# A short convolution ahead of a gated network: another start-up order, a band from 38 small matmuls, and another last store

## The chip, the cores and the metric

The kernel runs on one core of one Trainium2 chip. The metric is the device time of one execution in microseconds (us), as the median of several runs. A ratio is the mean time of one kernel's fast runs over that of the other's of the same rounds on the same chip, so it is not quite the ratio of the medians that stand beside it. Verdicts use 2% as the border between "same" and "faster" or "slower".

## The reference, cut to what matters

```python
w = softmax(weight, axis=-1)                    # 8 heads x 7 taps
# causal depthwise convolution over the sequence, one row of taps for each 24 channels
out = einsum('hk,bskhg->bshg', w, windows_of(x_pad))      # x: (8, 4160, 192)
x = out.reshape(33280, 192)
h = maximum(maximum(x @ w1, x @ w2), x @ w3)    # 192 -> 768
return h @ w_out                                # 768 -> 192, float32
```

## The kernel before

The 33,280 tokens are cut into 65 blocks of 512. For each block the kernel loads x, casts it to fp16, does the convolution as 40 small matmuls against a banded matrix (`band`), copies the result out of PSUM, repacks it by six DMAs, doubles it into the other 64 partitions by one more, and then runs two stages. The *first stage* is six steps: a step is six matmuls into two PSUM banks (w1-w3 and w2-w3), a relu on ACT and a maximum on DVE. The *second stage* multiplies the six h tiles, and the convolved x itself through the small matrix m16, into the output. Blocks 0 and 1 are started in another way, by a dense convolution of 120 matmuls (`conv_dense`) that needs no repacking.

The parts that the change touches are the band, the order of the loads, the order of the first blocks, and the last stores:

```python
wk = const.tile([1, NHEAD * KW], FP32)          # the 56 taps on one partition
load_x(0)
... w in six pieces (three of them, a third of the columns, first) ...
load_x(1)
nc.sync.dma_start(out=wos[:], ...)
for t in range(2, 6):
    load_x(t)
...
nc.tensor.matmul(wps, lhsT=ones[:], rhs=wk[:], ...)       # taps onto 128 partitions
... exp, sum, reciprocal, product; seven shifted products on DVE ...
for k in range(KW):                                       # seven 304-column matmuls
    nc.tensor.matmul(ps[:], lhsT=ident16[:], rhs=shifted[:, k, :, :], ...)
... casts of x0 and copies of w3 on ACT ...
for a in range(4):
    nc.scalar.copy(out=band[32 * a:32 * a + 32, :, 32 * a:32 * a + WIN], in_=ps[...])
...
for t in range(1, NB):                                    # the loop starts at block 1
    load_x(t + 7); cast_x(t + 5); double(t + 2)
    l1(t, 0)
    ... convolutions of two blocks in every second iteration, copies, repack ...
    st2(t - 1, 0, NJ)
    for j in range(1, NJ):                                # first and second stage interleaved
        l1(t, j)
        st2(t - 1, j, NJ)
    store(t - 1, 0, 4, (nc.gpsimd,))
for u in range(NJ):
    st2(NB - 1, u, NJ)                                    # with the last block's stores
```

The softmax here doesn't subtract the row's maximum and nothing guards it: scores larger than these inputs give would overflow.

## Time and profile before

| what | value | from |
|---|---|---|
| time | 483.85 us (483.21 to 484.04, 3 runs) | times |
| span of the profiled run, mean granted clock | 480.0 us, 0.993 | profile |
| first convolution starts | 10.75 us | chain in order of time |
| convolutions of the iteration of block 4 | 47.99 us | chain in order of time |
| two blocks of the loop | 13.95 us | 61.94 - 47.99, the same chain |
| last add on DVE ends | 474.16 + 0.35 = 474.51 us | timeline |

A time in the profile counts from the start of the span. "PE" is TensorE; a line number names a line of that kernel's own file, so the convolution of blocks 0 and 1 is L342 in one kernel and L310 in another; the tile (`D`) is the same. The lines that the prediction rests on are shown there. One more place of the profile of before is needed: its end. The timeline's columns are start, duration, engine, line, operation, tiles.

```profile
474.16 0.35 DVE L436 TENSOR_TENSOR o<-a,po 128x192 f32<-128x192 f32 x1 [0.17 <-ACT a L435]
474.55 0.66 ACTq L452 DMA_DIRECT2D out_dram<-o  x1
```

The last arithmetic ends at 474.51, and the span ends 5.49 us later.

### The profile page before, as it was taken

Reading aid. Unit: us, or ns where it says so; the run is one execution under the profiler, and the core shown is the slowest. Engines: PE = TensorE matmul, PEld = TensorE weight load, DVE = VectorE, ACT = ScalarE, POOL = GpSimd, SP = SyncE. Lnnn points to the kernel's source line nnn. Section 1 sums busy time; section 2 is a strip of 40 time slices with the busy share of each in tenths; the row PEclk is TensorE's granted clock in tenths of the full one; section 3 lists DMA queues with packets and bytes.
Section 4 is the critical chain, followed back from the end, with each engine's and each line's share of the span. In section 5 each row is a group of like instructions: output and inputs, shape, how many; then the busy total and the mean of one; then the engine's idle time right before and its main releaser. Section 6 shows DMA issues by size and latency. Waiting matters only on the chain.

```text
span 480.0 us, 21944 instructions
## 1 busy us (share of the span) xinstructions
PE 468.4 (98%) x9083; PEld 393.7 (82%) x9083; DVE 365.8 (76%) x609; ACT 327.1 (68%) x608; POOL 211.3 (44%) x341
## 2 busy tenths in 40 slices
PE   7899999999999999999999999999999999999994
PEld 3578888888888888888888888888888888888994
DVE  6667877778777877877787787778777777778774
ACT  5676667676666767666666766676676767667663
POOL 2654534553454355445435544543545354345210
PEclk9899999999999999999999999999999999999998
DMA  8877756665766665566666657566556666644312
GB/s 198 216 188 209 214 147 194 173 187 160 202 168 181 184 184 165 162 196 179 173 179 185 171 155 196 168 189 178 170 158 191 186 169 176 179 126 135 112 44 95
DMA packets 67603, 82.08 MB, mean 171 GB/s; under 512 B 9424, under 2 KB 55760, under 8 KB 67504
## 3 DMA queue, kind: packets, MB, share of 16 engines
q1 hardware_dynamic: 53934, 49.01, 40.6%
q0 software_dynamic: 13216, 31.38, 18.4%
q8 instruction: 71, 1.16, 1.1%
q10 hardware_dynamic: 354, 0.30, 0.2%
q14 instruction: 28, 0.23, 0.1%
HBM read 30.31 MB, written 25.56 MB: 116 GB/s over the span
## 4 chain that ended last, share of the span: by engine, by line
PE 96%; ACT 1%; DVE 1%; issue 0%; POOL 0%; POOLq 0%
PE lp L383 32%; PE po L426 30%; PE lq L383 26%; PE G L322 7%; PE D L342 1%; PE idle L196 1%; ACT r L387 0%; PE band_sum L245 0%; ACT band L268 0%; ACT w3h L262 0%; DVE h L388 0%; DVE xz L216 0%; PE pm L305 0%; PE wps L223 0%; DVE band L218 0%
## 5 line engine op out<-in xcount | busy, mean ns | idle before, releaser
L388 DVE TENSOR_TENSOR h<-r,lq 128x512 f16<-128x512 f16 x390 | 266.9, 685 | 101.8 <-ACT r L387 101.8
L387 ACT ACTIVATE r<-lp 128x512 f16<-128x512 f32 x390 | 232.7, 597 | 135.0 <-PE lp L383 89.8
L383 PE MATMUL lp<-yd,wd 64*128 64x512 f16 x1170 | 315.4, 376 | 0.1
L383 PE MATMUL lq<-yd,wd 64*128 64x512 f16 x1170 | 314.6, 375 | 0.0
L426 PE MATMUL po<-wo,h 64*128 64x192 f16 x3120 | 231.3, 243 | 0.1
L426 PEld LDWEIGHTS <-h 64*128 64x128 f16 x3120 | 186.9, 94 | 26.1 <-issue 0.3
L383 PEld LDWEIGHTS <-wd 64*128 64x128 f16 x2340 | 164.4, 94 | 20.9 <-issue 1.4
L452 POOL DMA_DIRECT2D out_dram<-o x64 | 50.7, 792 | 245.9 <-DVE o L436 229.1
L366 POOL DMA_DIRECT2D yd<-ys x189 | 95.5, 509 | 2.2 <-ACT ys L353 1.4
L426 PE MATMUL po<-m,yd 64*128 64x192 f16 x780 | 86.8, 243 | 0.0
L436 DVE TENSOR_TENSOR o<-a,po 128x384 f32<-128x384 f32 (+1 forms) x132 | 71.3, 541 | 0.6 <-ACT a L435 0.6
L146 POOL CAST x<-xf 112x960 f16<-112x960 f32 x62 | 61.6, 995 | 2.3 <-DMA xf<-in_x_dram 2.3
L435 ACT COPY a<-po 128x384 f32<-128x384 f32 (+1 forms) x132 | 61.8, 469 | 1.2 <-PE po L426 1.2
L426 PEld LDWEIGHTS <-yd 64*128 64x128 f16 x780 | 55.0, 94 | 8.1
L322 PEld LDWEIGHTS <-x 112*32 112x32 f16 x2480 | 30.0, 97 | 13.3 <-issue 13.1
L353 DVE CAST ys<-G 128x512 f16<-128x512 f32 x60 | 38.4, 681 | 0.0
L353 ACT CAST ys<-G 128x512 f16<-128x512 f32 x66 | 35.8, 589 | 2.2 <-PE G L322 0.9
L322 PE MATMUL G<-band,x 112*32 112x103 f16 (+1 forms) x2480 | 35.0, 210 | 0.0
L161 POOL CAST xz<-xf 112x240 f16<-112x240 f32 (+2 forms) x6 | 2.4, 450 | 11.3 <-DMA xf<-in_x_dram 11.3
L196 PE MATMUL idle<-idle 128*128 128x512 f16 x14 | 5.7, 546 | 1.2 <-DVE unit L212 1.2
L342 PE MATMUL D<-band,xz 112*32 112x103 f16 (+1 forms) x240 | 4.1, 240 | 1.0 <-ACT band L268 1.0
L342 PEld LDWEIGHTS <-xz 112*32 112x32 f16 x240 | 3.8, 114 | 1.5 <-issue 1.4
(50 smaller groups left out, 41.2 us busy)
## 6 DMA issues: line engine op xcount, KB each, us to landing
out_dram<-o POOLq DMA_DIRECT2D x64, 384.0 KB, 3.9
xf<-in_x_dram SPq DMA_DIRECT2D x57, 420.0 KB, 4.8
yd<-yd SPq DMA_DIRECT2D x63, 192.0 KB, 3.2
yd<-ys SPq DMA_DIRECT2D x63, 48.0 KB, 3.6
yd<-ys POOLq DMA_DIRECT2D x63, 48.0 KB, 3.3
xf<-in_x_dram SPq DMA_DIRECT2D x8, 252.0 KB, 3.1
yd<-ys SPq DMA_DIRECT2D x63, 32.0 KB, 3.2
yd<-ys POOLq DMA_DIRECT2D x63, 32.0 KB, 2.9
```

What stands on the lines that cost most here:

```text
L146: nc.gpsimd.tensor_copy(out=v[0:rl, q0:q1, :], in_=xf[0:rl, q0:q1, :])
L322: nc.tensor.matmul(G[i][32 * g:32 * g + 32, lo:hi], lhsT=x16[0:rlen, cb:cb + 32], rhs=band[0:rlen, h, cc:cc + hi - lo], start=True, stop=T ...
L342: nc.tensor.matmul(ps[32 * g:32 * g + 32, lo:hi], lhsT=xz[t][0:rlen, q, v, 32 * s:32 * s + 32], rhs=band[0:rlen, h, cc:cc + hi - lo], star ...
L353: copy(out=slots[t][:, i, :], in_=convs[t][i][:])
L366: (nc.sync, nc.gpsimd)[n % 2].dma_start(out=yd[r0:r0 + rows, c, :], in_=slots[t][s0:s0 + rows, half, :])
L383: nc.tensor.matmul(ps[i][:, 0:N], lhsT=wd[row, c, P * j:P * (j + 1)], rhs=y[row, c, 0:N], start=(c == 0), stop=(c == NC - 1))
L387: nc.scalar.activation(out=r[:, 0:N], in_=ps[0][:, 0:N], func=AF.Relu)
L388: nc.vector.tensor_max(out=hs[t][:, j, 0:N], in0=r[:, 0:N], in1=ps[1][:, 0:N])
L426: nc.tensor.matmul(ps[b0, i][:, s % 2, :], lhsT=a, rhs=b, start=first, stop=last)
L435: nc.scalar.copy(out=a[:, ss, :], in_=ps[s0, 0][:, ss, :])
L436: nc.vector.tensor_add(out=outs[t][:, s0:s + 1, :], in0=a[:, ss, :], in1=ps[s0, 1][:, ss, :])
L452: qs[i].dma_start(out=bass.AP(tensor=out.tensor, offset=r * D, ap=[[D, n], [step * D, s1 - s0], [1, D]]), in_=ob[p0:p0 + n, s0:s1, :])
```

## The change

The intent is to start real work earlier and to keep TensorE on the blocks that are already there: the band comes from 38 matmuls of 8 columns instead of seven DVE products and seven 304-column matmuls; x1 is loaded behind the first third of w; second stages 0 and 1 both run ahead of block 2; loads of x are issued one at a time, with four buffers instead of six; and the last store but one leaves through SP in two halves. The cuts leave out smaller changes that come with these: w is loaded and copied in thirds, the casts of x0 move from ACT to DVE and those of w3 to GpSimd, and the second stage of block 0 takes its terms in another order.

```diff
-    xfp = ctx.enter_context(tc.tile_pool(name="xfp", bufs=6))
+    xfp = ctx.enter_context(tc.tile_pool(name="xfp", bufs=4))
...
     load_x(0)
-    ... w in six pieces on two queues ...
+    load_w(0)
     load_x(1)
+    load_w(1)
+    load_w(2)
     nc.sync.dma_start(out=wos[:], ...)
-    for t in range(2, 6):
-        load_x(t)
+    load_x(2)
...
-    keep_warm(2)
-    nc.tensor.matmul(wps[:]..., lhsT=ones[:], rhs=wk[:], start=True, stop=True)
-    ... taps, shifted (7 products) ...
-    keep_warm(7)
-    for k in range(KW):
-        nc.tensor.matmul(ps[:], lhsT=ident16[:], rhs=shifted[:, k, :, :], ...)
-    keep_warm(3)
+    keep_warm(6)
+    nc.scalar.activation(out=wexp[:], in_=wk[:], func=AF.Exp, accum_out=wsum[:])
+    nc.vector.reciprocal(out=wrec[:], in_=wsum[:])
+    nc.vector.tensor_scalar(out=line[:, 31:31 + KW], in0=wexp[:], scalar1=wrec[:], ...)
+    for c in range(WIN):
+        nc.tensor.matmul(bps[:, c, :], lhsT=line[:, WIN - 1 - c:WIN + 31 - c],
+                         rhs=ident16[0:NHEAD, 0:NHEAD], start=True, stop=True)
+    keep_warm(4)
...
+    conv_dense(0, ...)
+    l1(0, 0); l1(0, 1); conv_dense(1, ...); l1(1, 0); l1(1, 1); l1(0, 2); l1(0, 3)
+    load_x(3, nc.scalar)
+    ... the other steps of blocks 0 and 1, st2(0, 0) ...
+    conv(2, PQ); evac(2, ...); repack(2)
+    load_x(4)
+    ... st2(0, 1) to st2(0, 3), l1(1, 5) ...
+    double(2)
+    cast_x(3)
+    conv(3, PQ); evac(3, ...)
+    load_x(5)
+    repack(3)
+    ... rest of st2(0), then all six of st2(1) ...
+    load_x(6); double(3)
-    for t in range(1, NB):
+    for t in range(2, NB):                     # block 2 without second-stage work between
...
+            if t == NB - 1 and j == 3:
+                store(t - 1, 0, 2, (nc.sync,))
+        if t == NB - 1:
+            store(t - 1, 2, 4, (nc.sync,))
-        store(t - 1, 0, 4, (nc.gpsimd,))
+        elif t > 2:
+            store(t - 1, 0, 4, (nc.gpsimd,))
```

## The prediction

> **What bounds the kernel now.** I read the page first (chain of work, 40 slices), then the windows of each engine, then the timeline of the first 48 us and of the last 13, because the change touches only those ends. The page's chain of work that ended last, by engine, and its slices of TensorE and granted clock:
>
> ```profile
> PE 96%; ACT 1%; DVE 1%; issue 0%; POOL 0%; POOLq 0%
> ...
> PE   7899999999999999999999999999999999999994
> ...
> PEclk9899999999999999999999999999999999999998
> ```
>
> TensorE owns 96% of the chain. Only the first two slices (24 us) and the last hold idle time. The windows (length, then busy us and instruction count of PE, PEld, DVE, ACT, POOL, then clock, DMA share, GB/s) say it in numbers:
>
> ```profile
> 0.00:10.70 10.70, 7.28 (x21) 3.06 (x22) 7.04 (x18) 5.40 (x13) 2.97 (x18) 1.00 0.84 196
> 10.70:33.10 22.40, 20.51 (x529) 13.97 (x530) 13.24 (x22) 15.10 (x26) 12.95 (x21) 0.92 0.78 192
> ...
> 47.10:466.90 419.80, 419.69 (x8143) 358.49 (x8139) 328.93 (x542) 292.23 (x542) 187.74 (x291) 1.00 0.59 170
> ```
>
> From 47 us to 467 us TensorE is busy 419.69 of 419.80 us, so nothing there can be won, and the diff leaves those matmuls as they are. So I predict the time at which a fixed milestone is reached: the first-stage matmuls of block 4 start, with convolutions 0 to 6, first stages 0 to 3 and second stages 0 to 2 done. Before, that is at 47.1 us (timeline; the two convolutions of that iteration follow at 47.92). The difference at this milestone, plus the tail, is the whole change.
>
> Real work starts late and then stutters. From the chain in order of time (start, us, what):
>
> ```profile
> 7.24 1.79 PE band_sum L245 x7
> 9.05 0.40 ACT band L268
> 9.46 0.40 ACT band L268
> 9.88 0.40 ACT band L268
> 10.29 0.41 ACT band L268
> 10.75 1.55 PE D L342 x107
> ...
> 14.71 1.47 ACT w3h L262
> 16.20 0.60 ACT r L387
> ```
>
> The first convolution starts at 10.75, when the fourth band copy ends; later a 1.47 us cast on ACT delays a relu and TensorE waits.
>
> A second limit matters. One first-stage step (six matmuls) takes TensorE 0.64 us, but its two PSUM banks come free only after the relu (0.60) and the max (0.69): in the timeline a step begins at 456.20 and its max ends at 458.36, 2.16 us. With two banks of each kind, steps without second-stage work between them run at about 2.16/2 = 1.1 us. In the loop second-stage matmuls (about 0.41 us per step) fill that hole, so a loop step takes 1.06.
>
> [...] the granted clock is 0.81, 0.50 and 0.84 in the 2 us windows from 18, 20 and 22 us, which is (0.38+1.00+0.32)/0.5 = 3.4 us at half rate. [...] Here the six 64-column transposes beginning at 17.57 took 0.33 us with latency[...]. [...] Here even the small pieces take 3 us and more from issue to landing:
>
> ```profile
> xf<-in_x_dram SPq DMA_DIRECT2D x57, 420.0 KB, 4.8
> yd<-yd SPq DMA_DIRECT2D x63, 192.0 KB, 3.2
> ...
> yd<-ys POOLq DMA_DIRECT2D x63, 48.0 KB, 3.3
> ```
>
> **The change part by part.**
>
> *Band.* Removed: ones, the K=1 product, the replicated exp, seven DVE products (2.79 us) and seven 304-column matmuls (1.98 us). Added: exp straight on the loaded weights, reciprocal, one product, 38 matmuls of 8 columns. Weights landed by 3.4 us before; exp 0.25 and two DVE steps of about 0.2 give the line at 4.1. [...] The four band copies stay, 1.65 us: first convolution at about 7.4 instead of 10.75. **Gain 3.3.**
>
> *Load order.* Bytes land at roughly 190 to 215 GB/s (3144 KB by 17.2 us before). After: x0 (420 KB) 4.6, first third of w (576 KB) 8.0, x1 10.0, the rest of w by 15.5, w_out 18.1, x2 20. Block 0's first step needs the third of w: copy, then a 0.96 us subtraction on DVE from 8.06 to 9.02, then the second convolution bank's copy, 0.69. So step (0,0) starts at 9.05 against 12.23. Still 3.2 ahead. x1 at 10.0 instead of 14.9 lets convolution 1 run at 11.5 to 13.1 instead of 18.9 to 21.4. **This removes the before kernel's worst hole.**
>
> *Where it is lost, 1: ACT and DVE.* From here I walked through each engine's instruction order with the durations above. ACT now carries half the x1 casts (0.96), two w3 copies (0.83 each), three w3 transposes' copies (0.48), the convolution copies and a DMA issue (about 0.6). Convolution 1's output is ready at 14.1 (TensorE idle from 13.1). Then ten first-stage steps follow with no second-stage work between them, at about 1.1 us each plus the small matrix products: last of them at 25.5. Second stages 0 and 1 can only begin there, since the former needs all six h tiles. So the order of blocks 0 and 1 bunches what the loop interleaves: ten steps cost 4 us more than their 0.64.
>
> *Loss 2: GpSimd order.* Convolution 2's second copy ends at 27.6. The cast of x3 stands behind GpSimd's three repack issues (3 x 0.51), so it runs 28.8 to 29.8; TensorE has only second-stage work up to 28.6. **1.3 us idle.**
>
> *Loss 3: one load at a time.* On SP, the doubling DMA of block 2 waits for the repack pieces to land (28.3 + 3.3 = 31.7), then needs 3.2: block 2's first step can start at about 35.0, while TensorE has finished second stage 1 at 34.0. **1.0 idle.** The load of x5 stands behind that doubling on SP: issued at 32.2, landed (4.5 to 4.8) at 36.9, cast 1.0, so convolution 5 starts at 38.0, while TensorE is free from 36.2. **1.8 idle.** Before, four loads of x were issued from 7.5 us and their casts were done by 24.
>
> *Loss 4: block 2 without second stages.* Second stage 1 is already done, so the remaining five steps of block 2 again take about 1.05 us each with nothing between: 38.6 to 43.6, **1.7 more** than their matmuls.
>
> Block 3 then takes 6.4 + 0.5 (one convolution): block 4 starts at 43.6 + 6.9 = 50.5 against 47.1, **+3.4 us**. Check by holes: start -3.3, and idle or half-filled time after it about 9.5 (1.1 + 2.6 net + 1.3 + 1.0 + 1.8 + 1.7) against about 4.7 before, which would give only +1.5. The step-by-step walk gives more because it also counts latencies between engines; I lean towards it.
>
> *Loop.* Four x buffers instead of six and a load one block later. A load issued in block t is needed by a cast at the start of block t+1 and by a matmul two to three blocks on: one block is 6.97 us, a landing 4.8. **Nothing.**
>
> *Tail.* The store of block 63 leaves by SP in two halves rather than by GpSimd at 472.90. It clears 192 KB out of the way of the last stores, which then finish as they do now, set by the last add at 474.16 and an ACT issue. **0.2 gain.**
>
> Sum: 483.85 + 3.4 - 0.2 = 487.0; weighted with the holes' +1.5, **486.6**.
>
> **The rivals.** (A) *The earlier start survives.* If the bunched steps run closer to 0.64 than to 1.1 us and the landings are nearer 2.5 than 3.3, the 3.3 us of the start stay: 481 to 483. For it: TensorE idles or runs cold for some 5 us between 10.7 and 33 before. Against: two banks of each kind, and a max that takes 0.69 by itself. (B) *A cold clock on top.* The hole around 36 to 38 us, with little work from 34 on, is longer than the one that halved the clock at 19 us before. A window of 3.4 us at half rate there costs up to 1.7 us, partly hidden since the steps wait anyway: 488 to 490. (C) *The 38 matmuls are slow.* [...] 4 us instead of 1.4, the convolution starts at 10, and nearly nothing is gained at the start: 488 to 489. (D) *Nothing visible:* the pieces cancel within a microsecond, 483 to 485.
>
> **Range and chances.** The late start is certain within 1 us. The losses depend on one chain (convolution 2's copy, repack, doubling, load, cast), which may shift by 1.5 us either way; the clock adds mostly upwards. I take 483.5 to 490.0 for 8 in 10. Two per cent is 9.7 us, more than the whole prologue has to give or lose by this reckoning: faster 0.01, same 0.96, slower 0.03.
>
> **What would show it.** Right: first convolution near 7.4 us; first-stage steps of blocks 0 and 1 about 1.1 us apart; TensorE waiting for GpSimd's cast before convolutions 3 and 5 and for the doubled block before block 2; block 4's first step at 49 to 52 us; the loop's two-block period still 13.95. Wrong: block 4's first step before 47 (A), the band matmuls taking over 3 us (C), a loop that has new holes from late loads, or a tail that moves by more than 0.5 us.

The sum came to 483.85 + 3.4 - 0.2 = 487.0 us, and weighted to 486.6. One term that it builds on: the estimate of 1.0 to 2.0 us for the 38 matmuls, which led from the line at 4.1 us to 5.6 and, with the band copies, to the first convolution at 7.4 and the gain of 3.3. The trace of before gives nearly the same by itself: its six transposes from 17.57 us take 0.33 us together, 55 ns each, and start 28 ns apart ((0.33 - 0.19)/5, one taking 0.19), so 38 such would take an estimated 1.1 to 2.1 us. Of the clock that trace shows one stretch at half rate ahead of the last matmul, from 19.22 to 22.64 us, after 3.41 us in which matmuls ran for 0.57 of the time. For rival C's slow matmuls no reason was shown; its 4 us are an assumption.

## The result

The changed kernel took **488.42 us** (488.02 to 489.74, 4 runs) beside 483.64 us (483.21 to 484.04, 4 runs) for the kernel before: ratio 1.0104, 95% interval 1.0082 to 1.0125. It is slower by 1.0%, which counts as the same at 2%. It lies inside the predicted range, and 1.8 us above the predicted time. All outputs are right.

The page of the changed kernel, first its slices, then the queue that brings instructions (packets, MB, share), then the chain by engine:

```profile
PE   7787999999999999999999999999999999999996
...
PEclk9898999999999999999999999999999999999999
...
q8 instruction: 71, 1.16, 1.1%
...
PE 92%; DMA 3%; issue 1%; ACT 1%; DVE 1%; SPq 1%; POOL 0%; DVEq 0%
```

TensorE's share of the chain fell from 96% to 92%; 3% went to DMA and 1% to "issue", time in which the engine waited for nothing that the profile shows. Nearly all of it is in the first four slices; 1.0 us of "issue" comes in the fifth, at 59.5 us. The windows of the changed kernel (length, busy us and count of PE, PEld, DVE, ACT, POOL, then clock, DMA share, GB/s) show where:

```profile
12.00:14.00 2.00, 0.00 (x0) 0.00 (x0) 0.64 (x1) 0.78 (x1) 0.82 (x1) 1.00 1.09 216
14.00:16.00 2.00, 1.80 (x85) 1.59 (x86) 0.94 (x2) 0.66 (x2) 0.00 (x0) 0.65 1.11 285
16.00:18.00 2.00, 2.00 (x12) 0.77 (x10) 0.68 (x2) 1.11 (x2) 0.15 (x1) 0.50 0.81 170
...
38.00:40.00 2.00, 0.00 (x0) 0.00 (x0) 0.53 (x1) 0.52 (x1) 0.69 (x1) 1.00 0.99 326
...
42.00:44.00 2.00, 2.00 (x13) 0.72 (x9) 1.52 (x3) 0.97 (x2) 1.35 (x3) 0.50 1.00 243
44.00:46.00 2.00, 2.00 (x14) 0.92 (x12) 0.90 (x2) 1.10 (x2) 0.66 (x1) 0.67 0.95 279
...
53.90:474.60 420.70, 419.70 (x8140) 357.94 (x8138) 329.12 (x542) 292.06 (x542) 187.61 (x291) 1.00 0.64 171
```

Two whole windows (12 to 14 and 38 to 40 us) hold no matmul, and each is followed by a stretch at half clock. The last line answers to 47.10 to 466.90 before: the same 419.70 us of TensorE in the loop, with 1.0 us idle in it. The chain in order of time (start, us, what) names the two holes:

```profile
10.75 0.56 PE D L310 x37
11.31 2.89 issue
14.20 1.68 PE D L310 x70
...
33.73 5.53 DMA xf<-in_x_dram
39.31 1.00 POOL x L146
40.35 0.64 PE G L290 x33
```

The first hole lies inside convolution 1, between two of its 120 matmuls, which all have the same inputs ready. The second is the load of x5 and its cast. The waits of TensorE up to 75 us (in total, times, longest):

```profile
PE G L290 <- POOL x L146: 4.0, 2, 2.4
PE D L310 <- issue: 2.9, 1, 2.9
PE po L395 <- issue: 1.0, 1, 1.0
```

The 4.0 are 1.58 ahead of convolution 3 and 2.43 ahead of convolution 5. The transfers themselves take about what they took (4.8, 3.2 and 3.3 us before); the last number is the median from issue to landing:

```profile
xf<-in_x_dram SPq DMA_DIRECT2D x56, 420.0 KB, 4.7
yd<-yd SPq DMA_DIRECT2D x63, 192.0 KB, 3.7
...
yd<-ys POOLq DMA_DIRECT2D x63, 48.0 KB, 3.5
```

At the end of the span the changed kernel is better than the prediction had it:

```profile
481.99 0.35 DVE L405 TENSOR_TENSOR o<-a,po 128x192 f32<-128x192 f32 x1 [0.17 <-ACT a L404]
482.38 0.71 ACTq L421 DMA_DIRECT2D out_dram<-o  x1
```

From the end of that add (482.34) to the end of the span (486.2) it takes 3.86 us, against 5.49 before.

**The balance of the two traces.** Convolution 0 starts at 6.72 instead of 10.75 (-4.0). The convolutions of block 4's iteration start at 54.79 instead of 47.99 (+6.8). Between these marks TensorE was idle 9.3 us after (3.57 in 6.72 to 16, 2.86 in 16 to 36, 2.91 in 36 to 53.9) and about 1.9 us before (20.51 busy of 22.40 up to 33.10, none after), which is +7.4. One stretch at half clock more is an estimated 1.7 (half of 3.4 us). -4.0 + 7.4 + 1.7 = 5.1; the other 1.7 of the 6.8 I put down to half-filled first-stage steps, by subtraction only. A wait of 1.0 us at 59.5 and the shorter end (-1.6) give 6.2, the difference of the spans.

### The profile page after: what moved, and what is told of

The parts are those of the page before. It is cut to its first block, busy times and chain, and to the rows that moved or that the text cites. A ratio compares the mean times of both kernels' runs of the same rounds, so it can differ in the third digit from the quotient of the medians.

```text
span 486.2 us, 21991 instructions
## 1 busy us (share of the span) xinstructions
PE 469.3 (97%) x9108; PEld 390.2 (80%) x9108; DVE 365.6 (75%) x605; ACT 324.5 (67%) x604; POOL 211.5 (44%) x340
## 3 DMA queue, kind: packets, MB, share of 16 engines
q8 instruction: 71, 1.16, 1.1%
## 4 chain that ended last, share of the span: by engine, by line
PE 92%; DMA 3%; issue 1%; ACT 1%; DVE 1%; SPq 1%; POOL 0%; DVEq 0%
PE lp L351 31%; PE po L395 29%; PE lq L351 25%; PE G L290 7%; DMA xf<-in_x_dram 1%; DMA ws<-in_moe_w_dram 1%; ACT r L355 1%; DMA yd<-ys 1%; DVE h L356 0%; PE D L310 0%; SPq L176 0%; DVE wd L245 0%; POOL x L146 0%; SPq L130 0%; ACT w3t L262 0%
## 5 line engine op out<-in xcount | busy, mean ns | idle before, releaser
L321 DVE CAST ys<-G 128x512 f16<-128x512 f32 x63 | 40.5, 683 | 3.9 <-PE G L290 3.9
L321 ACT CAST ys<-G 128x512 f16<-128x512 f32 x63 | 34.2, 588 | 6.6 <-PE G L290 5.0
L206 PE MATMUL idle<-idle 128*128 128x512 f16 x10 | 3.8, 529 | 1.2 <-DVE idle L201 1.2
L316 ACT CAST yd<-D 128x512 f16<-128x512 f32 x4 | 2.3, 586 | 3.6 <-PE D L310 3.6
```

Of the source, the lines that this page charges most:

```text
L321: copy(out=slots[t][:, i, :], in_=convs[t][i][:])
```

## The experiments

**The theory after the result.** (1) The hole of 2.9 us in convolution 1 is a late instruction fetch. The 71 packets of the instruction queue hold 1.16 MB, 16 KB each, and the page counts 18,216 matmuls and weight loads of TensorE (9108 of each); that is 257 rows to a packet, so I take a packet to be a block of 256 rows, an estimate from these counts. The hole comes after 447 recorded loads and matmuls. The DMA view has an instruction packet start at 11.48, and TensorE resumes at 14.20, 2.7 us later. The DMA share is 1.15 at that time: the packet would have to share the engines with the loads of w. (2) The load of x5, asked for behind the doubling of block 2, costs its wait of 2.4 us and the half clock after it. **The rivals:** the order of the second stages or GpSimd's order is at fault; or the hole is a wait for data that the profile missed.

### x45_early: x4 and x5 asked for right after x3

```diff
     load_x(3, nc.scalar)
+    load_x(4)
+    load_x(5)
...
-    load_x(4)
...
-    load_x(5)
```

> The changed kernel with the loads of x4 and x5 issued right behind that of x2 on SP, nothing else moved. My theory: the wait of TensorE for x5's cast before convolution 5 (2.43 us in the changed kernel) is gone or under 0.3, and the half-clock window that follows it (about 42 to 45 us) with it; the run is 2 to 3 us faster than the changed kernel, near 486. Rival: the doubling of block 3, or contention of these loads with those of the weights, takes the wait's place, and the run gains less than 1 us.

Measured: 483.76 us (482.57 to 484.82), ratio 1.0017, interval 0.9984 to 1.0051. Of the changed kernel's 1.04% it takes back 0.87%, some 4.2 us, more than I expected. The windows of this run show why:

```profile
42.00:44.00 2.00, 1.65 (x32) 0.73 (x34) 1.36 (x3) 1.16 (x3) 0.99 (x1) 1.00 1.12 282
44.00:46.00 2.00, 2.00 (x68) 1.51 (x55) 1.60 (x3) 1.27 (x3) 0.99 (x1) 1.00 1.10 251
```

The clock is 1.00 where it was 0.50 and 0.67, so both went (the clock records of the changed kernel have it at half from 41.91 to 45.32): the wait of 2.4 us and an estimated 1.7 us of half clock, together 4.1. The hole in convolution 1 stayed (2.60 us after the same 37 matmuls), and so did the wait for the cast of x3 (1.6). The loop's wait of 1.0 us is also absent from this trace, and the edit does not aim at it.

### cast3_first: GpSimd casts x3 ahead of its repack issues of block 2

```diff
     evac(2, 1, nc.vector.tensor_copy)
+    cast_x(3)
     repack(2)
...
-    cast_x(3)
     conv(3, PQ)
```

> The changed kernel with GpSimd's cast of x3 ahead of its repack issues of block 2. My theory: the wait before convolution 3 (1.58 us) vanishes, but the first step of block 2 still waits for its doubled block (near 36.5 us) and convolution 5 for x5 (near 40.3 us), so the time stays within 0.4 us of the changed kernel's 488.4. Rival, my prediction's way of adding: the wait counts in full, 1.3 to 1.6 us faster.

Measured: 488.36 us (485.64 to 489.42), ratio 1.0105, interval 1.0064 to 1.0145: nothing gained. The wait for the cast of x3 is gone, and TensorE waits 4.4 us for the doubling of block 2 in its place, with a half-clock stretch from 36.4 to 46.7 us. The wait for x3 was real, but something else stood right behind it.

### gate: later thirds of w, w_out and x2 held back until convolution 0 has given its first copy

```diff
-    load_w(1)
-    load_w(2)
-    nc.sync.dma_start(out=wos[:], ...)
-    load_x(2)
...
     conv_dense(0, (nc.scalar, nc.vector, nc.scalar))
+    gate = const.tile([1, 16], FP16)
+    nc.sync.dma_start(out=gate[:], in_=dense[0][0:1, 0, 0:16])
+    load_w(1)
+    load_w(2)
+    nc.sync.dma_start(out=wos[:], ...)
+    load_x(2)
```

> The changed kernel with the second and third thirds of w, w_out and x2 issued only after the first copy of convolution 0 (about 8 us; a 32-byte transfer on SP waits for it), so that fewer bytes stand in front of TensorE's next block of instructions. My theory: the 2.9 us hole in the middle of convolution 1 is a late instruction fetch behind the loads; it shrinks to under 1.2 us, the half-clock window after it shortens or goes, and the run is 1.5 to 3.5 us faster than the changed kernel. Rival: the hole has another cause (a wait the profile doesn't show, or the fetch takes its time whatever the queue), stays at 2.5 us or more, and the time is the same or worse.

Measured: 484.31 us (483.10 to 485.68), ratio 1.0030, interval 0.9994 to 1.0067. In the timeline convolution 1 now runs in one piece:

```profile
10.90 1.56 PE L306 MATMUL D<-band,xz 112*32 112x103 f16 x120
```

The instruction packet starts at 8.17 us instead of 11.48, and the DMA share is 0.04 from 8 to 10 us, where it was 1.15. TensorE's list is the same up to there. So with the loads held back the packet comes 3.3 us earlier and the hole of 2.9 us is gone: the loads delay the packet, and the packet makes the hole. The edit pays for it: the first step of block 1 then waits 1.5 us for ACT's copy of convolution 1, and half clock returns from 39.1 to 42.6 us.

### nowarm: no warming matmuls

```diff
-    keep_warm(6)
...
-    keep_warm(4)
```

> The changed kernel without its ten keep-warm matmuls (20 rows fewer in TensorE's list). Fetch theory: the hole in convolution 1 begins 10 matmuls later (after 47 of 120 instead of 37), because it stands at a fixed place in the instruction list, and ends at nearly the same time, 14.0 to 15.0 us. Rival: it stands at the same matmul of convolution 1 (tied to its data). In both, [...] the total is within 1 us of the changed kernel.

The clause that is cut was an estimate for convolution 0 that rested on no trace.

Measured: 484.07 us (483.04 to 484.38), ratio 1.0018, interval 0.9984 to 1.0051. The list is 20 rows shorter ahead of convolution 1, so the hole should come 10 matmuls later. The timeline has it there, after 47 instead of 37:

```profile
12.34 0.73 PE L308 MATMUL D<-band,xz 112*32 112x103 f16 x47
14.46 1.03 PE L308 MATMUL D<-band,xz 112*32 112x103 f16 x73 [1.39 <-issue]
```

Twenty rows fewer move the hole by ten loads and ten matmuls: its place is set by the count of instructions, not by the convolution's data. The time was a miss. I had expected it within 1 us of the changed kernel, and it was 4 us faster. The trace shows two things together: convolution 1 ends at 15.49 instead of 15.88, and neither half-clock stretch is there (recorded clock 1.00 in every window from its first record, at 12.33 us; the view prints 1.00 for the time before too, although convolution 0, which lies in it, took 2.77 us for its 120 matmuls instead of 1.55). Two stretches at an estimated 1.7 and the 0.4 make 3.8. Yet the run still waited 1.4 us for a doubling and 2.5 us for casts.

**What brings the half clock.** The kept traces answer this, though no run was made for it. In each trace the stretches at half clock begin a whole number of times 3.413 us after the first clock record: at 14.60 and 41.91 us in the changed kernel (3 and 11 such lengths after 4.36) and at 19.22 before (3 after 8.98), and each of these three lasts 3.413 us. So I cut each trace there into windows of that length, up to its last matmul, and took the share of each window in which a matmul was running. Half clock follows 13 of the windows at full clock; their shares are 0.05 to 0.50, and once 0.57 (the kernel before). It follows none of the other 1870, of which the lowest stand at 0.54. In the changed kernel the two windows are 11.19 to 14.60 us (0.15) and 38.50 to 41.91 us (0.45). In nowarm the waits are spread over more windows (the lowest 0.54, 0.59 and 0.62), and the clock holds. Where the windows lie differs from trace to trace (the first record stands at 4.36 to 13.41 us), so one kernel can meet a stretch in one run and miss it in the next. Of the four runs of gate, two have a mean clock of 0.999 and 1.000, which leaves no room for a stretch, and took 483.33 and 483.10 us; the other two (0.995 and 0.993) took 485.68 and 485.29 us.

### band_old: the changed kernel with the old band

```diff
-    line, the exp with its sum, the product, 38 matmuls, keep_warm(6), keep_warm(4)
-    cast_dense(0, (nc.vector.tensor_copy, nc.vector.tensor_copy))   # after the band copies
+    unit, ones, wps, taps, shifted, 7 matmuls, keep_warm(2), keep_warm(7), keep_warm(3)
+    cast_dense(0, (nc.scalar.copy, nc.scalar.copy))                 # ahead of the band copies
```

> The changed kernel with the old band only (product with ones, seven products, seven 304-column matmuls, 12 warming matmuls; x0's casts on ACT as before); everything else as changed. Instruction-fetch theory: TensorE's list has 56 rows fewer ahead of convolution 1 (40 instead of 96), so the hole should sit 28 matmuls further on (about matmul 65 of convolution 1), and as convolution 1 begins later while the fetch does not, it should be under 1 us. The first convolution is back at 10.5 to 11.5 us; of the 4.0 us of earlier start about half is then lost: 489.5 to 491 us. Rival: the earlier start is swallowed by later holes that the loads and the doubling set, so undoing the band costs under 0.7 us (488 to 489). Second rival: the start is worth its whole 4 us: 492 or more.

Measured: 489.06 us (488.66 to 490.94), ratio 1.0120, interval 1.0092 to 1.0147. The first convolution is back at 10.78. So 4.0 us of earlier start were worth 0.16% or 0.8 us, which the intervals do not separate from nothing: the first rival holds best. The two traces show what took the rest: against the changed kernel the hole is 0.9 us longer here, but the wait for x5 is 0.97 us instead of 2.43, one stretch at half clock (an estimated 1.7) is missing, and so is the loop's wait of 1.0. The place of the hole came as expected, after 64 matmuls of convolution 1 (expected about 65), but its length did not: 3.79 us, not under 1.

```profile
18.85 0.82 PE L327 MATMUL D<-band,xz 112*32 112x103 f16 x56 [3.79 <-issue]
```

I had taken it that the fetch would not begin later; the packet starts at 16.20 instead of 11.48. In these two traces the packet thus follows TensorE's own progress. Counting rows: the row one block before the hole (447 - 256 = 191) is reached at 11.6 us here and at 7.2 us in the changed kernel, so the packet comes 4.6 and 4.2 us after it; with the loads held back it comes 0.5 us after it (7.7 and 8.2 us in gate). That a packet is asked for at about row 190 of a block is my estimate from these rows, not something that a record says. The later packets agree: with blocks counted from the first row of the list, of the 71 in each of the 14 traces, 53 to 59 start before the 256th row of their block, and none before row 170.

### interleave: the second stage of block 1 back between the steps of block 2

```diff
-    for u in range(NJ):
-        st2(1, u, NJ)
...
-        if t == 2:
-            cast_x(6)
-        else:
-            st2(t - 1, 0, NJ)
+        if t == 2:
+            cast_x(6)
+        st2(t - 1, 0, NJ)
         for j in range(1, NJ):
             l1(t, j)
-            if t > 2:
-                st2(t - 1, j, NJ)
+            st2(t - 1, j, NJ)
```

> The changed kernel with the second stage of block 1 put back between the first-stage steps of block 2 (loads, band, casts as changed). My theory: block 2's first step waits for its doubled block either way (36.0 us in the changed kernel), so taking 2.4 us of work away from before that wait makes the wait 2.4 us longer, and the 1.7 us of half-empty steps after it are filled instead: 488.0 to 489.5, no gain. Rival, as the prediction's loss 4 read by itself would have it: the half-empty steps of block 2 cost 1.7 us, and interleaving gains them: about 486.7.

Measured: 489.50 us (488.67 to 493.21), ratio 1.0135, interval 1.0101 to 1.0168. No gain, as the theory had it. TensorE now waits 3.1 us for the doubling of block 2, for which the changed kernel shows no such wait: the second stage of block 1 had covered it.

### x45_gate and x45_nowarm: two edits that won, together

`x45_gate` is x45_early with gate; `x45_nowarm` is x45_early with nowarm; the diffs are those above.

> Both single edits that won: x4 and x5 asked for right after x3, and the later thirds of w, w_out and x2 held back until the first copy of convolution 0. If the two losses are separate (4.2 us for x5's late load with the cold window after it, 3.6 us for the fetch hole), the gains add up: 479 to 481 us, faster than both kernels. If both edits take away the same loss, the half-clock window after 40 us, the sum is no better than one: 483 to 484.5.

> x4 and x5 asked for right after x3, and no warming matmuls. Taking the warming away alone gave 4 us, which I had not expected. If that gain lies in the shorter hole of convolution 1 and in the clock of 14 to 18 us, it is separate from x5's load and adds to it: 479.5 to 481. If it lies in the half-clock window after 40 us that did not come, x4 and x5 early has it already: 483 to 484.

Measured: x45_gate 482.31 us (481.25 to 483.24), ratio 0.9973, interval 0.9947 to 1.0000; x45_nowarm 482.96 us (482.69 to 483.54), ratio 0.9988, interval 0.9961 to 1.0016. If the gains of x45_early (0.87%) and gate (0.74%) were separate, the first ratio would be 0.9943; if they were the same, 1.0017. It lies between, and both expectations for it missed. With intervals of 0.002 to 0.004 to either side of each ratio, separate gains are not excluded, so how much the two share is not measured. x45_nowarm comes nearest to the second of its expectations (483 to 484): most of what nowarm gained, x45_early has already. The recorded clock of x45_gate is 1.00 in every window up to 54 us, and what the two can share is the half clock near 40 us: the trace of x45_early has none there, and two of the four runs of gate had none at all. What each removes by itself is the hole and the wait. In x45_gate the DMA share is 0.07 from 8 to 10 us and the instruction packet starts at 8.3.

### x45_gate_c3 and x45_gate_c3_int: with the cast of x3 first, and with the interleaving

> x4 and x5 early, the later thirds of w held back, and also the cast of x3 ahead of GpSimd's three repack issues of block 2. With both edits before it TensorE still waited 1.6 us for that cast (29.8 us). Alone on the changed kernel this third edit gained nothing, as the wait moved to the doubling of block 2 and to x5. Now x5 no longer stands behind the doubling, but block 2's own doubling still does, and a cast ahead of the issues delays the repack by 1 us: I expect the 1.6 us to reappear as a wait of 1 to 2 us for the doubling, and the time within 0.7 us of the 482.3 (ratio 0.997) of the two edits. Rival: it adds up, 480.5 to 481.

> The three edits together and the second stage of block 1 put back between the steps of block 2. Theory (as seen in the interleave run): block 2 waits for its doubled block, so work taken away from before that wait lengthens it: 1 to 2 us slower than the three edits alone. Rival: with x5 early and the cast of x3 early the doubling is no longer late, and interleaving fills half-empty steps: 1 to 2 us faster, about 480.5.

Measured: 483.97 us (482.30 to 485.17), ratio 1.0026, interval 0.9997 to 1.0056; and 485.29 us (484.39 to 486.86), ratio 1.0055, interval 1.0025 to 1.0085. Neither adds to the two edits. The wait for the cast of x3 is again exchanged for one for the doubling (3.1 us in the first, 4.2 in the second). The first even has a ratio 0.5% above that of x45_gate, on another chip; that is more than the 0.7 us that I had allowed. Its profiled run, the fastest of the six, has a mean clock of 1.000, the other five 0.994 to 0.996.

### band_alone: the kernel before with the new band and nothing else

```diff
-    wk = const.tile([1, NHEAD * KW], FP32)
+    wk = const.tile([NHEAD, KW], FP32)
...
-    ... the old band, keep_warm(2), keep_warm(7), keep_warm(3) ...
+    ... the new band, keep_warm(6), keep_warm(4) ...
...
-        nc.scalar.copy(out=band[...], in_=ps[32 * a:32 * a + 32, :, :])
+        nc.scalar.copy(out=band[...], in_=ps[:].rearrange("p c h -> p h c"))
```

> The kernel before with the new band alone (38 small matmuls, 10 warming matmuls); loads, casts and the order of the blocks as before. The first convolution should start at 7 to 8 us instead of 10.75. My theory: the earlier start is worth next to nothing by itself, because the next thing the kernel before waits for is loads: its first step needs the parts of w (12.2 us) and convolution 1 needs x1 (landed 14.9, then its casts) and stands behind a 1.5 us cast on ACT: within 1 us of before, 483 to 484.5. Rival: ACT and DVE are freed 3 us earlier and the copies and casts that follow move up with the band, so 2 us or more are gained: 481 to 482.

Measured: 486.82 us (484.71 to 487.69), ratio 1.0073, interval 1.0041 to 1.0105: slower than before by 0.7%, clear of the noise though the same by the 2% border, which neither of my theories had. The first convolution starts at 9.11 only, since the band copies stand behind ACT's copy of w3, and it takes 2.77 us instead of 1.55. Convolution 1 starts where it did (18.89). In the profiled run, the fastest of its six, the loss comes in convolution 2:

```profile
20.28 0.40 PE L302 MATMUL G<-band,x 112*32 112x103 f16 x19
24.04 0.67 PE L302 MATMUL G<-band,x 112*32 112x103 f16 x21 [3.36 <-issue]
```

Up to there 351 matmuls and 352 weight loads are recorded, 703 rows. In the changed kernel it was 223 and 223 or 224, and in nowarm, x45_early, cast3_first, interleave, x45_nowarm and band_old as well. 703 - 447 = 256: the hole of band_alone is exactly one block of instructions further on. The waits in the loop fit too, if the few other rows of TensorE's list (semaphores and drains, 2 of them by the first hole) are counted. The changed kernel's wait of 1.0 us at 59.5 us comes after 990 + 991 + 4 = 1985 rows, and one of 1.4 us in gate at 304.7 us after 11,713; less the 449 rows of the first hole, these are 6 and 44 times 256. In the changed kernel the packet starts at 57.78 there, 2.75 us before TensorE resumes.

The kernel before has the same boundary: after 702 recorded rows, at 23.2 us, it waits 0.17 us, and tail_alone, which starts as it does, waits 1.0 us there.

```profile
PE pm L301 <- issue: 0.2, 1, 0.2
```

With the new band 97 recorded rows instead of 43 stand ahead of the first matmul of convolution 0. TensorE reaches the boundary at 20.7 us, in the middle of convolution 2, and waits for the packet that starts at 21.44.

### tail_alone: the kernel before with the new end and nothing else

```diff
             st2(t - 1, j, NJ)
-        store(t - 1, 0, 4, (nc.gpsimd,))
+            if t == NB - 1 and j == 3:
+                store(t - 1, 0, 2, (nc.sync,))
+        if t == NB - 1:
+            store(t - 1, 2, 4, (nc.sync,))
+        else:
+            store(t - 1, 0, 4, (nc.gpsimd,))
```

> The kernel before with the tail of the change alone: the store of the last block but one leaves through SP in two halves instead of GpSimd in one piece. In the profiles the time from the end of the last add on DVE to the end of the span is 5.5 us in the kernel before and in the run with the new band alone (both with the old tail), and 3.8 to 4.2 us in all kernels with the new tail. If the tail is what makes this difference, this kernel is 1.4 to 1.7 us faster than before: ratio 0.9965 to 0.9972, about 481.5 us. Rival, as the prediction had it: 0.2 us, ratio 0.9995 or above.

Measured: **480.77 us** (480.00 to 483.97) beside 483.45, ratio 0.9953, interval 0.9918 to 0.9988. It is faster than the kernel before by 0.5%, far less than 2%, and has the lowest ratio, though it is not told apart from x45_gate's 0.9973. In its trace the last add ends at 474.85 and the span at 478.8, which is 3.95 us against 5.49 before: 1.5 us of the 2.3 that the ratio gives are this, and the interval holds 1.5.

```profile
474.50 0.35 DVE L436 TENSOR_TENSOR o<-a,po 128x192 f32<-128x192 f32 x1 [0.17 <-ACT a L435]
```

Where the 1.5 us go is in the instruction rows of the kept traces, some of which the views leave out. The last store lands 2.9 us after the last add before, and 2.7 us after it here, so the last stores finish hardly sooner. But GpSimd's closing DRAIN (the last long row of its list) starts with the issue of GpSimd's last store and lasts 6.2 to 6.3 us in all 14 traces. Before, it runs from 472.88 to 479.21, while SP's closing drain ends at 477.98: the end of the kernel stands behind GpSimd for 1.2 us. Here GpSimd's last store is that of block 62, its DRAIN is over at 473.11, and the end follows SP's drain at 478.02.

## Why the prediction was right or wrong

"The same at 2%" and the range were right, and the predicted time was 1.8 us low. That the number came out so near is partly luck: the milestone came twice as late against before as predicted (+6.8 instead of +3.4 us), and the tail took 1.4 us of that back.

- **Band: gain 3.3.** The start was right and better than predicted (6.72 instead of 7.4), and rival C is out: the 38 matmuls took 1.14 us, 30 ns each. What failed is carrying this gain into the sum. The band_old run puts it at 0.8 us, not told apart from nothing, and band_alone shows that it can cost time by itself.
- **Small transfers.** The text has "even the small pieces take 3 us and more"; the 32 KB pieces on POOLq took 2.9 before. Nothing rests on it.
- **Load order: "removes the before kernel's worst hole".** This step failed. Convolution 1 started early (10.68) and broke off after 37 matmuls, for 2.9 us. The walk through the engines' orders looked at data only; instructions are transfers as well (71 packets of 16 KB in the changed kernel). The gate, nowarm and band_alone runs show the cause by its time and by its place.
- **Loss 1: steps about 1.1 us apart.** Right: from 15.82 to 24.19 us the first-stage steps of blocks 0 and 1 start 1.11 to 1.30 us apart, the first of them at half clock.
- **Loss 2: 1.3 before convolution 3.** Measured 1.58. Right in size, but it is no term that can be taken away alone: cast3_first gained nothing.
- **Loss 3: 1.0 for the doubling, 1.8 for x5.** No wait for the doubling is listed before block 2 in the changed kernel; its first step started at 36.04 instead of 35.0, later for the earlier holes. The wait for x5 was there with 2.43 us, and x45_early shows that mechanism right.
- **Rival B, a cold clock on top.** It came, from 41.9 to 45.3 us, after the hole at 38 to 40, and another stretch from 14.6 to 18.0 came after the fetch hole. Its 488 to 490 us is where the time fell. The prediction gave this its own rival and not a term of the sum.
- **Loss 4: 1.7 for block 2 without second stages.** The size was about right: the five steps took 5.2 us for the predicted 5.0, partly at half clock, and 4.7 in x45_gate at full clock. As a loss that one gets back by interleaving it is wrong: interleave gained nothing, since the doubling is what block 2 waits for.
- **Loop: nothing.** Right: 419.70 us of TensorE work as before, but for a wait of 1.0 us for instructions at 59.5 us in this run. The two-block period is 13.95 us in all pairs but the first, which has this wait.
- **Tail: 0.2.** The direction was right, the size off: 1.6 in the two profiles, and tail_alone shows it. The prediction said that the last stores "then finish as they do now", and they do: the last one lands 2.9 us after the last add in both kernels. What it did not have is GpSimd's closing DRAIN, 6.3 us from its last store's issue, which held the end back and no longer does once that store goes out a block earlier. The rows of the traces show this; no run tested the DRAIN by itself.
- **Milestone: block 4's first step at 50.5 (49 to 52).** It was at 53.9. +6.8 instead of +3.4, less 1.6 instead of 0.2 at the end.

What stays open: how much of the 6.8 us is half-filled steps, why the loop's fetches are late in some runs only, and what besides the end makes up the 2.3 us of tail_alone, if anything does.

## What to carry to other kernels

An earlier start is worth only what the next limit lets through (here 4.0 us were worth 0.8, not told apart from nothing); before counting a gain, walk on to the next load, the next DMA chain and the next block of instructions, and look whether a hole there will halve the clock as well, as it did after both holes of the changed kernel. When TensorE stops between matmuls of the same inputs with "issue" as the reason, count the rows of its list up to there, compare with the packets of the instruction queue, and see what the DMA engines are busy with. And test each part of a bundle alone: here the one that seemed worth 0.2 us won, and the one that seemed worth 3.3 us lost.
